# Reordering VectorE's preparing steps, the one-hot and mask step and the sums' transpose in a clustered attention kernel

## The chip, the cores and the metric

The kernel runs on one core of a Trainium2 chip. The metric is the device time of one execution in microseconds. Three runs of the kernel before took 787.32, 787.58 and 790.29 us, so the median is 787.58 us. All times below are microseconds unless ns stands beside them.

## The reference

Attention in which a query sees only the keys of its own cluster, and two dense layers behind it. The core of it:

```python
q_assign = np.argmax(np.einsum('bhsd,hcd->bhsc', q_n, c_n), axis=-1)
k_assign = np.argmax(np.einsum('bhsd,hcd->bhsc', k_n, c_n), axis=-1)
mask = q_assign[:, :, :, None] == k_assign[:, :, None, :]
scores = scale * np.matmul(q, k.transpose(0, 1, 3, 2))
scores = np.where(mask, scores, -1000000000.0)
attn = np.exp(scores - np.max(scores, axis=-1, keepdims=True))
attn = attn / (np.sum(attn, axis=-1, keepdims=True) + 1e-09)
out = np.matmul(attn, v)              # (2, 8, 768, 64)
x = out.transpose(0, 2, 1, 3).reshape(1536, 512)
h = x @ w_in                          # 512 -> 2048
x = softplus(h) @ w_out
h = x @ w_in2
out = (h * clip(h + 3, 0, 6) / 6) @ w_out2
```

There are 2 batches, 8 heads, 768 positions, head size 64 and 16 clusters; `argmax` takes the first of equal values. All of it is float32, and the kernel splits operands into a high and a low part and multiplies the parts.

## The kernel before

The attention works on eight pairs of heads, numbered 0 to 7. A pair takes twelve slots: two heads with six tiles of 128 queries each. In slot s the program issues, in this order: the exp of tile s+1 on ScalarE (line 424), the row maximum of tile s+2 on VectorE (`nm`, 416), the flips of tile s, the scores of tile s+3 on TensorE (408) and a piece of the product with the values (453). A flip is made of transposes of the exponentials on TensorE (`t`, 438) in two halves of three, and behind each half a high part on ScalarE (`pth`, 442) and a low part on VectorE (`ptl`, 443). The halves of `t` lie in two PSUM buffers, so each half waits for the low part of the same half one slot before. The scores have two PSUM buffers, so those of tile s+3 wait for the exp of tile s+1. Behind every third slot ScalarE copies a finished product (`xs`, 466 and 468).

Between these stand the steps that prepare a later pair. Each slot has seven positions, 0 to 6: position 1 lies behind the exp, 2 behind the row maximum, 3 between the two halves of the flip, 4 behind the flips, 5 behind the scores, 6 at the slot's end. A table written by hand, `at(slot, position, step, ...)`, says where each step is issued, and every engine runs its own instructions in that order. For pair n (2 to 7), o is the slot 12n - 12, and the twelve slots around o to o+11 are called the round of pair n here. Pair 1 has lines of its own in the table.

The steps that find a position's cluster: similarities (`psm`, 308), transposed back (`pbk`, 321), the maximum per group (`mx`, 330), equality with it (`eq`, 336), a rank multiplied on by GpSimd (343), the maximum of the ranks (`mx`, 348), the first of them as a one-hot row (`oh`, 353), its transposes on TensorE (`po`, 361), and from them the mask rows on ScalarE (`mk`, 367). `assemble` and `assemble_mask` copy the prepared query and key rows and the mask rows into `Q` and `K` by transfers issued on SP, whose queue also holds the pieces of the dense layers' weights (`fetch_part`). `psm`, `pbk`, `po` and the transposed sums share one PSUM buffer.

The sums of the exponentials of a finished pair are transposed on TensorE (`tot_flip`, `pb`, 483), copied by ScalarE (`tot_out`, `rT`, 488) and sent by SP; GpSimd scales the products by them and splits them into parts (`fin_hi` 511, `fin_lo` 517). GpSimd also splits the values (`p_values`, 377 and 378) and the centroids (290, 291) of the coming pair.

Pair 1's lines put the one-hot step and mask so:

```python
                    at(4, 4, p_first, n)
                    at(5, 3, p_onehot, n)
                    at(5, 6, p_mask, n)
```

Of the kernel before, what the change touches and what calls it, by code (L numbers as in the profile page):

```python
# [22 lines left out]
def cluster_attention_then_two_mlps(  # L23
# [149 lines left out]
    def attention():  # L173
        with ExitStack() as st, ExitStack() as st_ld, ExitStack() as st_ps:
# [347 lines left out]
            def at(s, where, fn, *a):  # L522
                extra.setdefault((s, where), []).append((fn, a))
# [5 lines left out]
            for n in range(NP):  # L529
                o = SL * n - SL  # L530
                if n > 1:
                    at(max(o + -15, 3), 6, load_qk, n, "q")
                    at(max(o + -13, 4), 6, load_qk, n, "k")
                    at(max(o + -9, 4), 5, p_centroids, n)
                    q0 = max(o + -11, 6)
                    at(q0, 1, p_split_hi, n, "q", 0)
                    at(q0, 2, p_split_lo, n, "q", 0)
                    at(o + -5, 1, p_split_hi, n, "q", 1)
                    at(o + -5, 2, p_split_lo, n, "q", 1)
                    at(o + -4, 1, p_split_hi, n, "k", 0)  # L540
                    at(o + -4, 2, p_split_lo, n, "k", 0)
                    at(o + -3, 5, p_split_hi, n, "k", 1)
                    at(o + -2, 1, p_split_lo, n, "k", 1)
                    at(o + -1, 4, p_sims, n, 0)
                    at(o + -1, 4, p_sims, n, 1)
                    at(o + 0, 1, p_sims, n, 2)
                    at(o + 0, 4, p_sims, n, 3)
                    at(o + 0, 4, p_sims_out, n)
                    at(o + 1, 1, p_back, n)
                    at(o + 1, 4, p_max, n)  # L550
                    at(o + 2, 2, p_equal, n)
                    at(o + 2, 4, p_rank, n)
                    at(o + 4, 2, p_best, n)
                    at(o + 5, 2, p_first, n)
                    at(o + 6, 3, p_onehot, n)
                    at(o + 6, 6, p_mask, n)
                    at(o + 4, 1, assemble, n, 0)
                    at(o + 7, 1, assemble_mask, n, 0)
                    at(o + 10, 5, assemble, n, 1)
                    at(o + 11, 4, assemble_mask, n, 1)  # L560
                    at(o + -3, 6, load_v, n)
                    at(o + 5, 5, p_values, n, 0)
                    at(o + 6, 4, p_values, n, 1)
                elif n:
                    at(0, 3, p_sims, n, 2)
                    at(0, 6, p_sims, n, 1)
                    at(1, 3, p_sims, n, 3)
                    at(1, 4, p_sims_out, n)
                    at(2, 3, p_back, n)
                    at(2, 6, p_max, n)  # L570
                    at(3, 2, p_equal, n)
                    at(3, 4, p_rank, n)
                    at(4, 2, p_best, n)
# [3 lines that stand above are left out]
                    at(4, 3, assemble, n, 0)  # L577
                    at(6, 3, assemble_mask, n, 0)
                    at(10, 5, assemble, n, 1)
                    at(11, 4, assemble_mask, n, 1)  # L580
                    at(1, 1, load_v, n)
                    at(7, 0, p_values, n, 0)
                    at(10, 3, p_values, n, 1)
                o += 2 * SL
                if n < NP - 1:
                    at(o + -2, 4, total, n)
                    at(o + 3, 0, tot_flip, n)
                    at(o + 3, 4, tot_out, n)
                    at(o + 4, 4, tot_spread, n)
                    at(o + 9, 4, fin_scale, n, 0)  # L590
                    at(o + 10, 4, fin_scale, n, 1)
                    at(o + 12, 5, fin_hi, n, 0)
                    at(o + 14, 5, fin_hi, n, 1)
                    at(o + 16, 2, fin_lo, n, 0)
                    at(o + 17, 3, fin_lo, n, 1)
                else:
                    at(o + -1, 1, total, n)
                    at(o + 1, 1, tot_flip, n)
                    at(o + 1, 1, tot_out, n)
                    at(o + 1, 5, tot_spread, n)  # L600
                    at(o + 4, 2, fin_scale, n, 0)
                    at(o + 4, 4, fin_hi, n, 0)
                    at(o + 4, 6, fin_lo, n, 0)
                    at(o + 4, 5, fin_scale, n, 1)
                    at(o + 4, 6, fin_hi, n, 1)
                    at(o + 6, 1, fin_lo, n, 1)
# [233 lines left out]
    with tc.manual_schedule():  # L840
        attention()
# [174 lines left out]
```

## Time and profile before

| | |
|---|---|
| time, median of 3 runs | 787.58 |
| time of the profiled execution | 787.78 |
| its span | 786.0 |
| TensorE busy, share of the span | 769.7, 98% |
| VectorE | 459.2, 58% |
| ScalarE | 416.1, 53% |
| GpSimd | 153.4, 20% |
| TensorE waiting for `K<-mk` transfers | 3.3 in 3 waits |

The attention stage takes about the first 260 us; the dense layers follow, and there TensorE runs without a gap that matters. The shares are means over both stages, so what a change in the attention stage does is read from windows and timelines of that stage. A row of a timeline gives start, duration, engine, line, operation, tiles and shapes, and in brackets how long its engine sat idle before it and for what; several alike are merged (x6), and then the duration is that of all of them. Durations of neighbours on one engine overlap a little.

### The profile page before, as it was taken

What the parts mean: (1) busy time and instruction counts of PE and PEld (TensorE: products, weight loads), DVE (VectorE), ACT (ScalarE), POOL (GpSimd) and SP (SyncE); (2) the same over time, 40 slices, a digit from 0 to 9 for tenths busy, and PEclk for the clock granted to TensorE, in tenths of its full rate; (3) what the DMA queues carried; (4) which work ended last, traced back from release to release, by engine and by line L of the source; (5) the groups of instructions that cost most, each with busy time, mean ns of one, the idle gap of its engine ahead of it and who ended that gap; (6) DMA issues with size and microseconds to landing.
All of it is one profiled execution on the core that took longest, in us unless ns stands there. A gap on an engine that the chain in (4) does not pass through costs nothing.

```text
span 786.0 us, 10568 instructions
## 1 busy us (share of the span) xinstructions
PE 769.7 (98%) x3841; PEld 642.6 (82%) x3841; DVE 459.2 (58%) x787; ACT 416.1 (53%) x830; POOL 153.4 (20%) x223
## 2 busy tenths in 40 slices
PE   7899999999999899999999999999999999999998
PEld 6688888898888688888888888888888888888886
DVE  6888878888888999821111267779842322232222
ACT  6898889889899666531212344455532322222221
POOL 4666757757433200000000000000000000000000
PEclk9999999999999999999999999999999999999999
DMA  6658667457372670000000356640000100010001
GB/s 188 168 144 220 148 163 182 106 136 167 86 213 93 218 285 0 1 1 0 1 1 27 106 169 208 189 159 0 1 1 0 54 1 0 1 54 0 1 1 54
DMA packets 39124, 69.75 MB, mean 89 GB/s; under 512 B 4480, under 2 KB 24096, under 8 KB 39072
## 3 DMA queue, kind: packets, MB, share of 16 engines
q1 hardware_dynamic: 39072, 69.08, 30.5%
q8 instruction: 30, 0.49, 0.3%
q14 instruction: 22, 0.18, 0.1%
HBM read 46.30 MB, written 3.19 MB: 63 GB/s over the span
## 4 chain that ended last, share of the span: by engine, by line
PE 84%; ACT 6%; DMA 4%; DVE 3%; issue 1%; SPq 1%; POOL 1%; ACTq 0%; DVEq 0%; POOLq 0%
PE h L169 32%; PE y L892 17%; PE y L890 16%; PE s L408 6%; PE t L438 5%; PE pv L453 5%; ACT pr L424 2%; ACT pth L442 2%; PE psm L308 2%; DMA K<-hik 2%; DMA q<-in_q 1%; DMA K<-mk 1%; SPq L397 1%; DMA Q<-loq 1%; DVE nm L416 0%
## 5 line engine op out<-in xcount | busy, mean ns | idle before, releaser
L169 PE MATMUL h<-xhi,pi 128*128 128x512 f32 x768 | 238.8, 392 | 2.2 <-DVE pi L144 2.2
L169 PEld LDWEIGHTS h<-xhi,pi 128*128 128x128 f32 x768 | 143.7, 188 | 34.3 <-DVE pi L144 3.0
L871 DVE TENSOR_TENSOR glo<-g,ghi 128x512 fp32r<-128x512 f32 x96 | 66.4, 692 | 146.2 <-ACT ghi L858 117.4
L169 PE MATMUL h<-xlo,pi 128*128 128x512 f32 x384 | 150.0, 391 | 0.0
L892 PE MATMUL y<-po,ghi 128*128 128x512 f32 x384 | 118.9, 391 | 0.0
L890 PE MATMUL y<-ghi,po 128*128 128x512 f32 x384 | 118.8, 391 | 0.0
L443 DVE TENSOR_TENSOR ptl<-t,pth 128x384 fp32r<-128x384 f32 x192 | 97.8, 550 | 31.0 <-ACT pth L442 30.6
L864 DVE SCALAR_TENSOR_TENSOR g<-u,h 128x512 f32<-128x512 f32 x48 | 33.0, 688 | 127.1 <-ACT u L860 127.1
L860 ACT ACTIVATE u<-h,half 128x512 f32<-128x512 f32 x48 | 32.9, 686 | 128.3 <-PE h L169 128.0
L408 PE MATMUL s<-K,Q 128*128 128x256 f32 (+1 forms) x384 | 90.8, 357 | 6.0 <-DMA K<-mk 3.3
L442 ACT ACTIVATE pth<-t 128x384 fp32r<-128x384 f32 x192 | 85.1, 487 | 16.8 <-PE t L438 16.2
L416 DVE TENSOR_REDUCE nm<-s 128x1 f32<-128x768 f32 x96 | 90.7, 945 | 4.5 <-PE s L408 4.5
L424 ACT ACTIVATE pr<-s,nm 128x768 f32<-128x768 f32 x96 | 86.5, 902 | 3.4 <-DVE nm L416 3.0
L438 PE MATMUL t<-ident,pr 128*128 128x128 f32 x576 | 87.0, 279 | 0.6 <-DVE ptl L443 0.2
L857 ACT ACTIVATE g<-h 128x512 f32<-128x512 f32 x48 | 28.5, 594 | 110.8 <-PE h L169 110.8
L169 PEld LDWEIGHTS h<-xlo,pi 128*128 128x128 f32 x384 | 72.1, 188 | 15.6
L892 PEld LDWEIGHTS y<-po,ghi 128*128 128x128 f32 x384 | 72.1, 188 | 15.6
L890 PEld LDWEIGHTS y<-ghi,po 128*128 128x128 f32 x384 | 72.0, 188 | 15.6
L408 PEld LDWEIGHTS s<-K,Q 128*128 128x128 f32 x384 | 65.8, 189 | 18.1 <-ACT pr L424 4.9
L438 PEld LDWEIGHTS t<-ident,pr 128*128 128x128 f32 x576 | 64.8, 140 | 17.4 <-DVE ptl L443 13.3
L892 PE MATMUL y<-po,glo 128*128 128x512 f32 x192 | 75.1, 391 | 0.0
L890 PE MATMUL y<-glo,po 128*128 128x512 f32 x192 | 75.0, 391 | 0.0
(123 smaller groups left out, 941.5 us busy)
## 6 DMA issues: line engine op xcount, KB each, us to landing
ri<-in_moe_w_in SPq DMA_DIRECT2D x29, 512.0 KB, 4.7
ro<-in_moe_w_out SPq DMA_DIRECT2D x29, 512.0 KB, 4.5
K<-hik SPq DMA_DIRECT2D x31, 192.0 KB, 4.8
Q<-hiq SPq DMA_DIRECT2D x15, 384.0 KB, 5.0
Q<-loq SPq DMA_DIRECT2D x16, 192.0 KB, 4.3
v<-in_v SPq DMA_DIRECT2D x8, 384.0 KB
rsb<-row SPq DMA_DIRECT2D x16, 192.0 KB, 3.9
out<-o SPq DMA_DIRECT2D x12, 256.0 KB, 2.0
```

The costliest lines, as they stand in the source:

```text
L169: nc.tensor.matmul(hs[n][:, :TB], w[:, c, :], x[c][:, cols], start=(c == 0 and i == 0), stop=(c == NC - 1 and i == 2))
L408: nc.tensor.matmul(ps[:, n0:n1], Q[i][:, u, j * P:(j + 1) * P], K[i][:, u, n0:n1], start=(u == 0), stop=(u == 1),)
L416: nc.vector.tensor_reduce(nm, st_s[t][:, :S], AX.X, ALU.max, negate=True)
L424: nc.scalar.activation(pr, st_s.pop(t)[:, :S], AF.Exp, bias=st_p[t], accum_out=sums_of[n][:, i, j:j + 1])
L438: nc.tensor.transpose(pt[:, c * P:(c + 1) * P], pr[:, kt * P:(kt + 1) * P], ident)
L442: last_flip[:] = [nc.scalar.activation(dh, src, AF.Copy)]
L443: nc.vector.tensor_tensor(dl, src, f32(dh), ALU.subtract)
L453: nc.tensor.matmul(st_v[h][:, :HALF], vs[:, kt, i, :], st_t[h][u][:, kt, :], start=(kt == 0 and u == 0), stop=(kt == NJ - 1 and u == 1),)
L864: nc.vector.scalar_tensor_tensor(t["g"], t["u"], 1.0, t["h"], ALU.min, ALU.mult)
L871: nc.vector.tensor_tensor(t["glo"], t["g"], f32(t["ghi"]), ALU.subtract)
L890: nc.tensor.matmul(y[:, :TB], w[:, e, :], x, **fl)
L892: nc.tensor.matmul(y, x[:, e * P:(e + 1) * P], w.rearrange("p c e -> p (c e)"), **fl)
```

## The change

Nothing is added or taken away; entries of the table move. For pairs 2 to 7 the equality, the maximum of ranks and the first-index step go from position 2, in front of a slot's low parts, to position 4, behind them (the latter two one slot earlier); the rank moves one position on; the one-hot transposes and the mask copy move from slot o+6 to slot o+5, the mask's transfers from (o+7, 1) to (o+6, 3); and the transpose of the sums goes from the head of slot o+3 to behind its scores.

```diff
-                    at(o + 2, 2, p_equal, n)
-                    at(o + 2, 4, p_rank, n)
-                    at(o + 4, 2, p_best, n)
-                    at(o + 5, 2, p_first, n)
-                    at(o + 6, 3, p_onehot, n)
-                    at(o + 6, 6, p_mask, n)
+                    at(o + 2, 4, p_equal, n)
+                    at(o + 2, 5, p_rank, n)
+                    at(o + 3, 4, p_best, n)
+                    at(o + 4, 4, p_first, n)
+                    at(o + 5, 3, p_onehot, n)
+                    at(o + 5, 6, p_mask, n)
...
-                    at(o + 7, 1, assemble_mask, n, 0)
+                    at(o + 6, 3, assemble_mask, n, 0)
...
-                    at(o + 3, 0, tot_flip, n)
-                    at(o + 3, 4, tot_out, n)
+                    at(o + 3, 5, tot_flip, n)
+                    at(o + 3, 6, tot_out, n)
```

On VectorE, this is what stands from slot o+1 (`mx` from `pbk`) to slot o+6 in the round of pair 2 before, with a slot's two low parts in one row:

```order
 L330 TENSOR_REDUCE mx<-pbk 128x24
 L416 TENSOR_REDUCE nm<-s 128x1
+L443 TENSOR_TENSOR ptl<-t,pth 128x3x128 x2
 L336 TENSOR_TENSOR eq<-pbk,mx 128x384
-L443 TENSOR_TENSOR ptl<-t,pth 128x3x128 x2
-L416 TENSOR_REDUCE nm<-s 128x1
-L443 TENSOR_TENSOR ptl<-t,pth 128x3x128 x2
-L416 TENSOR_REDUCE nm<-s 128x1
-L348 TENSOR_REDUCE mx_950<-eq 128x24
-L443 TENSOR_TENSOR ptl<-t,pth 128x3x128 x2
-L416 TENSOR_REDUCE nm<-s 128x1
-L353 TENSOR_TENSOR oh<-eq,mx_950 128x384
```

Rows with a minus are where they stood before: each preparing step lies between a row maximum and the low parts. The rows that follow now:

```order
+L416 TENSOR_REDUCE nm<-s 128x1
+L443 TENSOR_TENSOR ptl<-t,pth 128x3x128 x2
+L348 TENSOR_REDUCE mx_918<-eq 128x24
+L416 TENSOR_REDUCE nm<-s 128x1
+L443 TENSOR_TENSOR ptl<-t,pth 128x3x128 x2
+L353 TENSOR_TENSOR oh<-eq,mx_918 128x384
+L416 TENSOR_REDUCE nm<-s 128x1
```

Each step has changed places with the low parts and the row maximum: it lies behind the low parts and in front of the next row maximum, and `oh` stands one pair of low parts nearer to the start of the round.

On TensorE, slot o+5 of the same round now, from its flips to the values' product (before, its six transposes stood in one row without the `po` rows between them, which came one slot later):

```order
 L438 MATMUL t<-ident,pr 128x128 x3
 L361 LDWEIGHTS oh
 L361 MATMUL po<-identb,oh 128x128
 L361 LDWEIGHTS oh
 L361 MATMUL po<-identb,oh 128x128
 L361 LDWEIGHTS oh
 L361 MATMUL po<-identb,oh 128x128
 L438 MATMUL t<-ident,pr 128x128 x3
 L408 MATMUL s<-K_156,Q_154 128x512 x2
 L408 MATMUL s<-K_156,Q_154 128x256 x2
```

The one-hot transposes of the round stand between the two halves of the flip of slot o+5, one slot earlier than before and one VectorE row behind the step that makes `oh`.

## Rows read from the trace of the kernel before

**Rows 1.** Windows, one round each (engine busy, count; clock, DMA).

```profile
46.74:76.61 29.87, 28.93 (x188) 25.55 (x188) 25.87 (x46) 26.67 (x61) 18.45 (x24) 1.00 0.80 213
76.61:106.21 29.60, 28.90 (x189) 25.57 (x187) 24.46 (x44) 25.84 (x60) 20.21 (x27) 1.00 0.68 172
106.21:135.48 29.27, 29.05 (x188) 25.53 (x187) 24.44 (x44) 25.95 (x61) 20.19 (x27) 1.00 0.64 157
```

**Rows 2.** Timeline, TensorE, round of pair 4 (start, duration).

```profile
117.10 1.01 PE L438 MATMUL t<-ident,pr 128*128 128x128 f32 x6
...
119.38 1.01 PE L438 MATMUL t<-ident,pr 128*128 128x128 f32 x6
...
121.67 0.96 PE L438 MATMUL t<-ident,pr 128*128 128x128 f32 x6
122.09 0.31 PEld L438 LDWEIGHTS t<-ident,pr 128*128 128x128 f32 x3 [0.15 <-DVE ptl L443]
...
127.38 0.97 PE L408 MATMUL s<-K,Q 128*128 128x512 f32 x4 [0.21 <-ACT pr L424]
```

**Rows 3.** Timeline, VectorE, same round.

```profile
116.04 0.55 DVE L336 TENSOR_TENSOR eq<-pbk,mx 128x384 f32<-128x384 f32 x1
116.50 1.01 DVE L443 TENSOR_TENSOR ptl<-t,pth 128x384 fp32r<-128x384 f32 x2
...
119.70 0.95 DVE L416 TENSOR_REDUCE nm<-s 128x1 f32<-128x768 f32 x1
120.57 0.54 DVE L348 TENSOR_REDUCE mx<-eq 128x24 f32<-128x384 f32 x1
121.03 1.01 DVE L443 TENSOR_TENSOR ptl<-t,pth 128x384 fp32r<-128x384 f32 x2
...
122.82 0.55 DVE L353 TENSOR_TENSOR oh<-eq,mx 128x384 bf16<-128x384 f32 x1
```

**Rows 4.** Timeline, ScalarE, same round.

```profile
117.23 0.48 ACT L466 ACTIVATE xs<-pv 64x384 f32<-64x384 f32 x1
...
118.24 0.88 ACT L442 ACTIVATE pth<-t 128x384 fp32r<-128x384 f32 x2
...
122.21 0.96 ACT L442 ACTIVATE pth<-t 128x384 fp32r<-128x384 f32 x2 [0.41 <-PE t L438]
```

**Rows 5.** Timeline, VectorE and TensorE, slots 5 to 7 of round 1.

```profile
31.57 0.55 DVE L353 TENSOR_TENSOR oh<-eq,mx 128x384 bf16<-128x384 f32 x1
...
32.17 0.17 PEld L361 LDWEIGHTS <-oh 128*128 128x128 bf16 x3 [0.29 <-DVE oh L353]
...
32.35 0.50 PE L438 MATMUL t<-ident,pr 128*128 128x128 f32 x3
...
37.62 0.95 PE L408 MATMUL s<-K,Q 128*128 128x512 f32 x4
```

**Rows 6.** Timeline, GpSimd, round of pair 4.

```profile
116.67 1.00 POOL L343 TENSOR_TENSOR eq<-eq,tiew 128x384 f32<-128x384 f32 x1 [1.81 <-DVE eq L336]
117.61 0.50 POOL L511 CAST xhi<-xs 128x384 fp32r<-128x384 f32 x1
118.29 1.01 POOL L471 TENSOR_TENSOR xs<-xs,xs 128x384 f32<-128x384 f32 x1 [0.18 <-ACT xs L468]
...
120.36 1.99 POOL L517 TENSOR_TENSOR xlo<-xs,xhi 128x384 fp32r<-128x384 f32 x2
...
122.88 1.37 POOL L378 TENSOR_TENSOR vs<-v,vs 128x384 fp32r<-128x384 f32 x1
```

**Rows 7.** Timeline, GpSimd and VectorE, round of pair 7.

```profile
210.52 0.51 POOL L377 CAST vs<-v 128x384 fp32r<-128x384 f32 x1
210.63 0.81 DVE L353 TENSOR_TENSOR oh<-eq,mx 128x384 bf16<-128x384 f32 x1
```

**Rows 8.** TensorE's waits over the span (total, times, longest).

```profile
PE s L408 <- DMA K<-mk: 3.3, 3, 2.1
```

**Rows 9.** Timeline, SP's queue in round 3.

```profile
97.34 1.55 SPq L102 DMA_DIRECT2D ro<-in_moe_w_out  x3
```

## The prediction

> **What bounds the kernel now.** I read the page first: TensorE is nearly never idle, and after about 260 us its order is untouched by the change, so only the attention stage can move. Then I cut that stage at the same instruction of successive rounds with the windows view. A round (twelve slots, one head pair) takes 29.87, 29.60 and 29.27 us [rows 1]; ScalarE is busy for 25.95 of the last and VectorE for 24.44, so neither is full, and the granted clock is 1.00 throughout. The reader should see that the first two rounds are longer by 0.60 and 0.33 though their work is the same: these are the rounds in which scores wait for a mask transfer [rows 8]. Third, the timeline of one round, engine by engine. Below I use the round of pair 4: the flips of its slots o+3, o+4 and o+5 start at 117.10, 119.38 and 121.67, the scores of slot o+7 at 127.38 [rows 2]. A flip (the transposes of line 438) needs the PSUM half that VectorE's low part of the slot before has read, and low parts need ScalarE's high parts. The loop TensorE, ScalarE, VectorE, TensorE is what ends each slot, and the wait that ends last changes from slot to slot.
>
> **The change part by part.** It adds and removes no instruction. Six rounds change, those of pairs 2 to 7; pair 1 has lines of its own.
>
> *Equality, rank and second maximum behind the low parts.* Before, `eq` at 116.04 held up the low parts at 116.50 [rows 3], and the flips of slot o+3 were stretched to 1.01, waiting 0.36 for them [rows 2]. Now the low parts start 0.46 earlier and that stretch should go. It is worth nothing, because what is late next is in the same slot: ScalarE's two `xs` copies from 117.23 hold the high parts until 118.24 [rows 4], whatever VectorE does, and the low parts behind them release the flips at 119.38 [rows 2] as before. I take 0 per round; if that cover were absent it would be 0.36. One slot on, `mx` moves ahead of the row maximum, and the order becomes 0.46 of `mx`, 0.87 of `nm`, low parts, the same sum between two low parts: they stay at 121.03 [rows 3]. The row maximum ends 0.46 later, and the exp that reads it can be late by that at most; ScalarE idled 0.41 right behind that exp [rows 4], so this is hidden but for 0.05. `eq` starts 0.93 later, behind the low parts, and so does the rank on GpSimd: it ends at 116.67 + 0.93 + 1.00 = 118.60 [rows 6], over 1 us before `mx` asks for it at 119.70.
>
> *The sums' transpose behind the scores.* It costs TensorE the same, one place later. ScalarE's copy `rT` stands behind high parts that start at 118.24 and take 0.88 [rows 4]; by their end the flips and scores of the slot are long through, and the transpose with them. 0; SP's row transfer and the queue behind it start as before. Had ScalarE to wait, exp and the flips behind it would be late by what is missing of one transpose, a few tenths.
>
> *First-index and one-hot one slot earlier.* This is where I find the cost. Each VectorE row starts some 0.08 before the one ahead of it ends. `oh` now stands directly behind the low parts of slot o+4, so it starts at 121.03 + 1.01 - 0.08 = 121.96 instead of 122.82 and ends 0.55 later, at 122.51 [rows 3]. But its transposes moved by a whole slot, between the two flips of slot o+5. The second flip was free to go at 122.09 [rows 2]; now it stands behind transposes that wait for `oh`. Round 1 already has this arrangement and shows its price: `oh` from 31.57 ends at 32.12, TensorE waits 0.29 for it, and the second flip goes at 32.35, 0.23 behind the end of `oh` [rows 5]. So here: 122.51 + 0.23 = 122.74, against 122.09, 0.65 late. Does it come back? ScalarE has no slack from there on: `xs` and mask copy fall between this flip and the scores of slot o+7, in either order. Before, the way from the second flip to those scores took 127.38 - 122.09 = 5.29; in round 1, with the mask copy where the change puts it, 37.62 - 32.35 = 5.27 [rows 2, 5]. Equal, so the flip's lateness arrives whole. Six rounds: 6 x 0.65 = 3.9. Bounds: 0 if `oh` is there in time, 0.65 plus what follows if not.
>
> *What `oh` meets there.* `oh` reads two SBUF tensors. In round 7 it took 0.81 instead of 0.55: a cast on GpSimd had begun 0.11 earlier, and `oh` ended 0.41 behind the cast's end, as if it had stood still until then [rows 7]. In the other order, `oh` at 122.82 and GpSimd's L378 at 122.88, it was L378 that took 1.37, where the rank took 1.00 for the same size [rows 6]. So whichever starts second waits. At its new place `oh` meets the pair of L517 instructions: 120.36 to 122.35 before [rows 6]. The rank's delay moves them: rank to 118.60, then the addition (which waited for ScalarE until 118.29), then the pair, about 0.3 later, 120.6 to 122.6. `oh` at 121.96 falls inside the second one and waits until 122.6, ends at 123.0 instead of 122.5: 0.5 more for the flip, all of it on the same path. The pair stands there in the rounds of pairs 3 to 6; in that of pair 2 a short cast stands there, and in that of pair 7 the small centroid splits are missing, so the pair is through earlier. Bounds 0 (a gap) and 1.0 (all of one L517) a round; I take 0.5 for four and 0.2 for two, an estimate nearest to the row of round 7: 2.4.
>
> The Trainium skill ("SBUF — State Buffer", section "Who interferes with whom") says that a VectorE instruction with two SBUF inputs contends with a GpSimd instruction that reads SBUF, since its second input comes through a shared read interface, and that who issues first holds it for the whole instruction. By that rule the sum keeps the 2.4, without it it loses them; rows 6 and 7 agree with it in both directions.
>
> *Mask one slot earlier, and its transfers ahead of one weight piece.* In rounds 2 and 3 the mask's transfers stood behind three weight transfers that took SP 1.55 [rows 9], not behind the mask copy; one of the three now goes behind them, so masks land about 0.5 earlier while TensorE comes later by the above. Those waits go, and what shows is the undisturbed round: 0.60 + 0.33 = 0.9 gained [rows 1]. The wait of 2.1 in rows 8 belongs to round 1 and stays. In rounds 4 to 7 nothing waited there: 0.
>
> Sum: +3.9 + 2.4 - 0.9 = +5.4. The profiled execution took 787.78 (span 786.0 and 1.78 around it), 0.2 above the median shown, 787.58. From that median: 793.0.
>
> **The rivals.**
> A. The wait for `oh` comes, the meeting with GpSimd does not (the two slip past each other by a few tenths): +3.9 - 0.9 = +3.0, 790.6. For it: GpSimd's place is worked out over five instructions. Against it: `oh` is 0.4 inside the second L517 and 0.6 ahead of its end.
> B. The other side, not slower: the low parts no longer stand behind the preparing steps, and VectorE gets ahead so far that `oh` ends before the first flip of slot o+5 does, near 122.1. Then the stretch of 0.36 in six rounds and the 0.9 of mask waits are gained: -2.2 - 0.9 = -3.1, 784.5. It decides at `oh` starting 0.4 earlier than I put it. For it: three of the four steps do leave the low parts' way. Against it: `xs` at 117.23 fixes when the low parts of slot o+3 can start, and the chain behind is VectorE without a gap.
> C. The mask copy ahead of exp counts a second time: exp and with it the scores of slot o+6 come 0.56 later, and those of o+7 once more. +0.56 in six rounds on top: 5.4 + 3.4 = +8.8, 796.4. Against it: the equal 5.29 and 5.27.
>
> **How the numbers follow.** My forecast gets 0.50, A 0.32, B 0.10, C 0.08. For A the range must reach down to 789, for half of C and for a full meeting in all rounds (0.5 more in five) up to 795.5; below lies B with a bit of A, above most of C. Half a per cent, 3.9 us, is about what a measurement of this kernel can tell from no change; the bounds are 783.6 and 791.5. Slower: nine tenths of my forecast, a fifth of A, all of C, 0.59. Faster: a third of B and little else, 0.04. The rest, 0.37, is the same.
>
> **What would show it.** In the changed profile, round 4: flips of slot o+3 no longer stretched, yet those of o+4 where they were; a new TensorE wait for `oh` in rounds 2 to 7, 0.6 to 1.1 each between two flips of slot o+5; `oh` at about 1.0 instead of 0.55 in four rounds and starting during an L517; no wait of scores for `K<-mk` but round 1's; rounds of about 30.4. `oh` at 0.55 means A, no wait for `oh` means B, and then I was wrong; scores of slot o+6 waiting 0.5 for exp mean C.

## The result, and the profile after

The changed kernel took 794.22 us (median of 5 runs, 792.47 to 795.57), the kernel before 787.81 beside it (5 runs, 787.32 to 790.29). The ratio is 1.0068 with a 95% interval of 1.0052 to 1.0083, so the change costs 5.4 us (4.1 to 6.5); the two medians lie 6.4 apart, at the upper end of that. The prediction was 793.0 in a range of 789.0 to 795.5, slower the likeliest. The profiled execution took 792.47 with a span of 790.7, 4.7 more than the one of before.

The windows of rounds 2, 3, 4 and 7, cut at the same instruction as [rows 1]:

```profile
46.50:76.61 30.11, 29.38 (x188) 25.59 (x187) 26.00 (x46) 27.04 (x62) 18.37 (x24) 1.00 0.78 207
76.61:107.01 30.40, 29.32 (x188) 25.71 (x187) 24.90 (x43) 26.20 (x61) 20.02 (x27) 1.00 0.69 177
107.01:137.37 30.36, 29.28 (x188) 25.69 (x187) 24.88 (x43) 26.20 (x61) 20.05 (x27) 1.00 0.61 148
198.10:227.96 29.86, 29.28 (x188) 25.70 (x187) 24.38 (x43) 26.20 (x61) 11.06 (x13) 1.00 0.47 100
```

Against [rows 1] rounds 2, 3 and 4 are 0.24, 0.80 and 1.09 longer. Rounds 5 and 6 cut the same way are 1.10 longer each, round 7 (29.27 before) 0.59. Together 4.92. The stretch ahead of them is 0.24 shorter, which leaves 4.7: the whole difference of the two spans.

TensorE's waits over the span (total, times, longest):

```profile
PE po L361 <- DVE oh L353: 4.6, 6, 0.9
...
PE s L408 <- DMA K<-mk: 1.9, 1, 1.9
```

The wait for `oh` is new, one in each of six rounds: 0.64 in round 2, 0.89 or 0.90 in rounds 3 to 6, and 0.38 in round 7, where the prediction said 0.6 at least. Of the three waits of [rows 8] only round 1's is left. TensorE in the round of pair 4, against [rows 2]:

```profile
117.63 0.82 PE L438 MATMUL t<-ident,pr 128*128 128x128 f32 x6
...
120.18 1.01 PE L438 MATMUL t<-ident,pr 128*128 128x128 f32 x6
...
122.47 0.51 PE L438 MATMUL t<-ident,pr 128*128 128x128 f32 x3
123.86 0.34 PE L361 MATMUL po<-identb,oh 128*128 128x128 bf16 x3 [0.89 <-DVE oh L353]
...
123.99 0.31 PEld L438 LDWEIGHTS t<-ident,pr 128*128 128x128 f32 x3
...
129.31 0.94 PE L408 MATMUL s<-K,Q 128*128 128x512 f32 x4
```

The flips of slot o+3 are no longer stretched (0.82 for 1.01). Those of o+4 still are, and stand where they stood: 120.18 is 119.38 plus the 0.80 by which the round starts later. In slot o+5 the one-hot transposes stand between the halves and wait 0.89, and the second half goes at 123.99. That is 1.10 behind its place before (122.09 + 0.80). From there to the scores of slot o+7 it takes 5.32, 5.29 before: the lateness arrives whole, within 0.03. VectorE, same round, against [rows 3], with the one-hot of rounds 2 and 7 around it:

```profile
62.26 0.80 DVE L353 TENSOR_TENSOR oh<-eq,mx 128x384 bf16<-128x384 f32 x1
...
117.77 0.54 DVE L336 TENSOR_TENSOR eq<-pbk,mx 128x384 f32<-128x384 f32 x1
...
120.50 0.54 DVE L348 TENSOR_REDUCE mx<-eq 128x24 f32<-128x384 f32 x1
120.96 0.95 DVE L416 TENSOR_REDUCE nm<-s 128x1 f32<-128x768 f32 x1
121.83 1.01 DVE L443 TENSOR_TENSOR ptl<-t,pth 128x384 fp32r<-128x384 f32 x2
122.75 1.05 DVE L353 TENSOR_TENSOR oh<-eq,mx 128x384 bf16<-128x384 f32 x1
123.73 0.94 DVE L416 TENSOR_REDUCE nm<-s 128x1 f32<-128x768 f32 x1
...
213.85 0.55 DVE L353 TENSOR_TENSOR oh<-eq,mx 128x384 bf16<-128x384 f32 x1
```

The one-hot takes 1.05 in round 4 (1.06 in rounds 3, 5 and 6), 0.80 in round 2 and 0.55 in round 7. GpSimd, rounds 4 and 7, against [rows 6]:

```profile
118.39 1.01 POOL L343 TENSOR_TENSOR eq<-eq,tiew 128x384 f32<-128x384 f32 x1 [2.30 <-DVE eq L336]
119.36 1.01 POOL L471 TENSOR_TENSOR xs<-xs,xs 128x384 f32<-128x384 f32 x1
...
121.41 1.98 POOL L517 TENSOR_TENSOR xlo<-xs,xhi 128x384 fp32r<-128x384 f32 x2
123.33 0.83 POOL L377 CAST vs<-v 128x384 fp32r<-128x384 f32 x1
...
211.43 1.98 POOL L517 TENSOR_TENSOR xlo<-xs,xhi 128x384 fp32r<-128x384 f32 x2
213.35 0.51 POOL L377 CAST vs<-v 128x384 fp32r<-128x384 f32 x1
213.93 1.33 POOL L378 TENSOR_TENSOR vs<-v,vs 128x384 fp32r<-128x384 f32 x1
```

The pair of L517 ends at 121.41 + 1.98 = 123.39. The one-hot, begun at 122.75, ends at 123.80, 0.41 behind that, the distance of [rows 7]. The cast behind the pair, 0.51 otherwise, takes 0.83: it waits for the one-hot in its turn. In round 7 the pair is through at 213.41, before the one-hot begins at 213.85; there the one-hot is first, and it is L378, begun at 213.93, that takes 1.33, where the rank took 1.01. ScalarE, round 4, against [rows 4]:

```profile
118.03 0.48 ACT L466 ACTIVATE xs<-pv 64x384 f32<-64x384 f32 x1
...
119.04 0.87 ACT L442 ACTIVATE pth<-t 128x384 fp32r<-128x384 f32 x2
...
122.00 0.90 ACT L424 ACTIVATE pr<-s,nm 128x768 f32<-128x768 f32 x1 [0.28 <-DVE nm L416]
...
124.58 0.49 ACT L442 ACTIVATE pth<-t 128x384 fp32r<-128x384 f32 x1 [1.07 <-PE t L438]
...
125.52 0.90 ACT L424 ACTIVATE pr<-s,nm 128x768 f32<-128x768 f32 x1
```

`xs` and the high parts behind it stand 0.80 later than before, so the cover named for slot o+3 was there. The exp now waits 0.28 for the row maximum behind `mx`, and the idle 0.41 that followed it is gone. What is new is 1.07 for the second half of the flip. SP in round 3, against [rows 9]:

```profile
97.29 1.06 SPq L102 DMA_DIRECT2D ro<-in_moe_w_out  x2
98.44 1.20 SPq L397 DMA_DIRECT2D Q<-mk  x2
99.69 1.22 SPq L397 DMA_DIRECT2D K<-mk  x2
100.95 0.58 SPq L102 DMA_DIRECT2D ro<-in_moe_w_out  x1
```

One of the three weight pieces has gone behind the mask's transfers, as worked out.

### The profile page after: what moved, and what is told of

It reads as the page before. It is cut to its first block, busy times and chain, and to the rows that moved or that the text cites. A ratio compares the mean times of both kernels' runs of the same rounds, so it can differ in the third digit from the quotient of the medians.

```text
span 790.7 us, 10574 instructions
## 1 busy us (share of the span) xinstructions
PE 771.3 (98%) x3841; PEld 643.7 (81%) x3841; DVE 460.6 (58%) x787; ACT 418.0 (53%) x830; POOL 153.2 (19%) x223
## 4 chain that ended last, share of the span: by engine, by line
PE 85%; ACT 7%; DVE 6%; issue 1%; POOL 0%; DMA 0%; SPq 0%; ACTq 0%; DVEq 0%; POOLq 0%
PE h L169 32%; PE y L892 17%; PE y L890 16%; PE pv L453 6%; PE t L438 6%; PE s L408 5%; ACT pth L442 2%; PE psm L308 2%; ACT pr L424 2%; DVE ptl L443 2%; ACT xs L468 1%; DVE nm L416 1%; DVE oh L353 1%; ACT xs L466 1%; PE warm L245 0%
## 5 line engine op out<-in xcount | busy, mean ns | idle before, releaser
L438 PE MATMUL t<-ident,pr 128*128 128x128 f32 x576 | 85.4, 277 | 1.2 <-DVE ptl L443 0.2
```

The source lines that it names most:

```text
L438: nc.tensor.transpose(pt[:, c * P:(c + 1) * P], pr[:, kt * P:(kt + 1) * P], ident)
```

## The experiments

Each was timed in turn with the kernel before on the same chip, and its ratio is to that. Rounds are cut here from the first similarities (`psm`) of one to the next, from each kernel's profiled execution; rounds 5 to 7 are not in the table. The ratios also hold the clock dip told of at the end, which falls in round 1 of some executions; the rounds of the table lie behind it.

| kernel | rounds 2, 3, 4 | ratio | 95% interval |
|---|---|---|---|
| before | 29.82, 29.59, 29.27 | | |
| changed | 30.11, 30.39, 30.36 | 1.0068 | 1.0052 to 1.0083 |
| one-hot back | 29.85, 30.13, 30.10 | 1.0038 | 1.0026 to 1.0051 |
| one-hot alone | 30.75, 30.76, 30.73 | 1.0095 | 1.0081 to 1.0109 |
| sums alone | 29.84, 29.49, 29.27 | 0.9997 | 0.9986 to 1.0009 |
| centroids behind | 30.13, 29.89, 29.87 | 1.0037 | 1.0022 to 1.0051 |
| one-hot behind scores | 29.75, 29.78, 29.77 | 1.0044 | 1.0031 to 1.0056 |
| back, centroids behind | 29.92, 29.61, 29.60 | 1.0023 | 1.0010 to 1.0035 |
| mask on VectorE | 29.95, 29.73, 28.88 | 0.9994 | 0.9985 to 1.0004 |
| combined | 28.90, 28.89, 28.92 | 0.9973 | 0.9963 to 0.9984 |
| combined, values later | 28.91, 28.89, 28.89 | 0.9959 | 0.9945 to 0.9972 |
| values later alone | 29.81, 29.52, 29.27 | 0.9981 | 0.9972 to 0.9989 |

**One-hot back.** The changed kernel, with the one-hot's transposes, the mask and its transfers where they were.

```diff
-                    at(o + 5, 3, p_onehot, n)
-                    at(o + 5, 6, p_mask, n)
+                    at(o + 6, 3, p_onehot, n)
+                    at(o + 6, 6, p_mask, n)
...
-                    at(o + 6, 3, assemble_mask, n, 0)
+                    at(o + 7, 1, assemble_mask, n, 0)
```

> The changed kernel with the one-hot transposes, the mask copy and the mask's transfers back in slots o+6 and o+7; VectorE's preparing steps stay behind the low parts, the sums' transpose behind the scores. Theory 1 (the cost is TensorE's wait for the first-index step between two flips, and only that): no wait of po for oh in rounds 2 to 7, mask waits of rounds 2 and 3 as before, the time of the kernel before, 787.8, ratio 1.000. Theory 2 (oh in front of the row maximum, and held up by GpSimd, is a second path of nearly the same length: the row maximum of slot o+5 ends 0.8 later, the exp that reads it starts at about the row maximum's end + 0.1 instead of 123.06, and ScalarE has no slack behind it): rounds 4 to 6 longer than 29.27 by 0.7 to 0.9, round 7 by 0.4, in round 2 the lateness hides in the mask wait; together +3 to +4, 791, ratio 1.004. Oh still takes 1.05 in rounds 3 to 6 in both.

The ratio is 1.0038: no wait for `oh` is left, and yet rounds 4 to 6 are 0.83 to 0.86 longer than before. Its timelines, VectorE and then ScalarE, round 4:

```profile
122.58 1.06 DVE L353 TENSOR_TENSOR oh<-eq,mx 128x384 bf16<-128x384 f32 x1
123.57 0.94 DVE L416 TENSOR_REDUCE nm<-s 128x1 f32<-128x768 f32 x1
```

```profile
121.83 0.90 ACT L424 ACTIVATE pr<-s,nm 128x768 f32<-128x768 f32 x1 [0.29 <-DVE nm L416]
...
124.61 0.90 ACT L424 ACTIVATE pr<-s,nm 128x768 f32<-128x768 f32 x1 [0.81 <-DVE nm L416]
```

This is a second path, which the prediction does not have (the expectation names it). The one-hot now stands ahead of a row maximum, that maximum ends late, and the next exp waits 0.81 for it. ScalarE idles 0.29 + 0.81 = 1.10 in this stretch, 0.41 before [rows 4], so 0.69 of the 0.83 is there.

**One-hot alone.** The kernel before with only the three lines of that diff, in the other direction: one-hot, mask and transfers one slot earlier.

> The kernel before with only the one-hot transposes, the mask copy and the mask's transfers one slot earlier. Theory 1 (the second flip of slot o+5 starts 0.23 behind the end of oh, and its lateness arrives whole): oh stays at 122.82 to 123.37 of round 4, the flip goes at 123.6 instead of 122.09, each of six rounds 1.5 longer, less 0.9 for the mask waits of rounds 2 and 3: +8, 796, ratio 1.010; po waits for oh about 1.2 six times. Rival (what costs is VectorE's steps behind the low parts and the meeting with GpSimd; the one-hot transposes alone are short and TensorE catches up): within 1 us of the kernel before, 787 to 789, and oh at 0.55 as before in both.

1.0095, as expected. Without the earlier `mx` and first-index step the one-hot comes later, and TensorE, round 4 of this kernel, waits longer for it:

```profile
125.69 0.34 PE L361 MATMUL po<-identb,oh 128*128 128x128 bf16 x3 [1.25 <-DVE oh L353]
```

Rounds 4 to 6 are 1.46 longer than before, 1.10 in the changed kernel. So the moved VectorE steps soften what the one-hot's move costs, by 0.36 a round; moved without it they cost 0.83, as one-hot back shows. The two costs do not add.

**Sums alone.** The kernel before with only the last two lines of the change.

> The kernel before with only the sums' transpose and its copy behind the scores of slot o+3. My working: 0; ScalarE never waits for the transpose, rounds of 29.27 stay, 787.8, ratio 1.000 within 0.001. Rival (the copy rT now waits for TensorE and everything on ScalarE behind it, and SP's row transfer and mask transfers behind that, come later): a ScalarE wait of rT on pb of some tenths in each round, +1 to +2 in all.

0.9997: nothing that the interval can tell, as expected.

**Centroids behind.** The changed kernel with GpSimd's four short centroid splits two slots later, so that the pair L517 is through before the one-hot begins.

```diff
-                    at(max(o + -9, 4), 5, p_centroids, n)
+                    at(max(o + -7, 4), 4, p_centroids, n)
```

> The changed kernel with the centroid splits of the next pair moved behind the two low parts of the outputs on GpSimd, so that these end about 1.1 earlier and short operations of about 0.2 stand where oh comes; the other engines keep their order. Theory of the shared path (oh waits while a GpSimd instruction that began first runs): oh falls from 1.05 to 0.55 to 0.75 in rounds 3 to 6, po waits 0.4 to 0.6 there instead of 0.9, each of the four rounds 0.35 to 0.5 shorter: 1.4 to 2.0 less than the changed kernel, rounds 4 to 6 at 29.9 to 30.0 instead of 30.37, ratio to before about 1.0045. Rival (oh is long because of what it reads or because of its place behind the low parts): oh stays at 1.05 and rounds at 30.37, ratio 1.0068.

1.0037, a little less than expected. GpSimd, VectorE and TensorE in its round 4:

```profile
120.69 1.99 POOL L517 TENSOR_TENSOR xlo<-xs,xhi 128x384 fp32r<-128x384 f32 x2
```

```profile
123.12 0.55 DVE L353 TENSOR_TENSOR oh<-eq,mx 128x384 bf16<-128x384 f32 x1
```

```profile
123.73 0.34 PE L361 MATMUL po<-identb,oh 128*128 128x128 bf16 x3 [0.39 <-DVE oh L353]
```

The one-hot takes 0.55 again, TensorE's wait falls from 0.89 to 0.39, and rounds 4 to 6 are 0.48 or 0.49 shorter than in the changed kernel. That is the meeting, by itself. What is left over the kernel before, 0.60 to 0.62 in each of these rounds, goes with the place of the one-hot and its transposes.

**One-hot behind the scores.** The changed kernel with the transposes two positions later.

```diff
-                    at(o + 5, 3, p_onehot, n)
+                    at(o + 5, 5, p_onehot, n)
```

> The changed kernel with the one-hot one step later only, behind the scores of its slot, so that the transposed one-hot is copied by ScalarE where it is copied in the changed kernel. Theory (two paths: TensorE's wait for the one-hot, and the exp of slot o+6 that comes behind the late row maximum): no wait of po for oh is left, but the maximum still comes behind the one-hot, at about 124.0 against 123.1 before, so that rounds 4 to 7 take about 29.6 us (before 29.27): some 1.2 to 1.4 us over the kernel before, ratio 1.0015. Rival (the earlier place of the mask's copy on ScalarE is the cost): rounds stay near 30.4, ratio 1.007. Rival (only the wait of po costs anything): ratio 1.000.

1.0044: missed, it should have been 1.0015. Rounds 4 to 6 are 0.50 longer than before where 0.35 was expected, and ScalarE in round 5 shows a wait that the expectation does not have:

```profile
156.25 0.67 ACT L367 ACTIVATE mk<-po,mbi,msc 128x384 fp32r<-128x384 bf16 x1 [0.40 <-PE po L361]
```

Behind the scores the transposes are late for the mask's copy, and ScalarE waits for them instead. Round 7, cut at its flips, is 0.52 longer, so the rounds account for about 2.1 us of the 3.5. The rest goes with the clock dip told of below: 5 of the 6 runs have a mean clock of 0.998 or less, and the sixth took 789.86, 2.0 over the runs of the kernel before that have more (median 787.88). The rival that the earlier mask copy is the cost falls: it is as early here as in the changed kernel, and the rounds are 0.6 shorter.

**Back, centroids behind.** Both edits at once: one-hot back, centroids two slots later.

> The changed kernel with the one-hot's transposes, the mask and its transfers put back where the kernel before has them (as in e1_onehot_back), and besides GpSimd's work on the centroids moved two slots later (as in e4_centroids_behind), so that the one-hot no longer begins during a GpSimd instruction. Theory: the one-hot takes 0.55 us instead of 1.06, so that the row maximum behind it is 0.5 less late: rounds 4 to 7 of about 29.65 us, ratio 1.002, against 1.0038 without the second move. Rival (the maximum's lateness is not what costs e1 its 3 us): ratio 1.0038 again.

1.0023, as expected: rounds 4 to 6 are 0.30 to 0.33 longer than before, 0.5 less than without the centroids' move. The late row maximum is shown as the second path: shorten the one-hot ahead of it, and the round gets that much shorter. Against centroids behind (0.60 to 0.62) it also shows what the earlier place of transposes and mask adds to that path: 0.3 a round (0.26, changed kernel against one-hot back, where the one-hot takes 1.06).

**Mask on VectorE.** The kernel before with the mask made by VectorE from round 2 on, and the two steps at earlier positions of the same slot (the expectation says that nothing else moves; these positions do).

```diff
-                nc.scalar.activation(mk, d["po"][:, :HALF], AF.Identity, bias=mbi, scale=msc)
+                if n < 2:
+                    nc.scalar.activation(mk, d["po"][:, :HALF], AF.Identity, bias=mbi, scale=msc)
+                else:
+                    nc.vector.tensor_scalar(mk, d["po"][:, :HALF], msc, mbi, ALU.mult, ALU.add)
...
-                    at(o + 6, 3, p_onehot, n)
-                    at(o + 6, 6, p_mask, n)
+                    at(o + 6, 1, p_onehot, n)
+                    at(o + 6, 2, p_mask, n)
```

> The kernel before with the transposed one-hot copied (and made into the mask) by VectorE instead of ScalarE from round 2 on, nothing else moved. It asks whether ScalarE has slack in a round. Theory (it has none, its 29.27 us are the round): rounds 4 to 7 become shorter by part of that copy's 0.67, to about 28.8; rounds 2 and 3 stay as they are, bound by the mask's transfers; about 1.7 us less than the kernel before, ratio 0.998. Rival (TensorE or VectorE sets the round): rounds of 29.3 or more, ratio 1.000 or above.

0.9994, and the interval holds 1: the total decides nothing. The rounds do: 4 to 6 are 0.36 to 0.39 shorter, near the expected 28.8, and 2 and 3 are 0.13 and 0.14 longer. The windows of rounds 3 and 5 of this kernel:

```profile
79.50:109.20 29.70, 28.66 (x189) 25.46 (x188) 24.93 (x44) 25.41 (x59) 20.18 (x27) 1.00 0.70 176
138.10:167.00 28.90, 28.89 (x189) 25.44 (x188) 24.84 (x45) 25.54 (x60) 20.15 (x27) 1.00 0.61 146
```

With that copy gone from ScalarE, TensorE is busy for 28.89 of 28.90. So ScalarE had no slack for that copy where it stood; the copy's engine and its place changed together, and no run parts them. That TensorE now sets the round is read from its busy time alone, which was already 29.05 of 29.27 [rows 1].

**Combined.** The last kernel, with the mask's transfers right behind the mask and three weight pieces behind them.

```diff
-                    at(o + 7, 1, assemble_mask, n, 0)
+                    at(o + 6, 3, assemble_mask, n, 0)
...
-                        at(12 * f + 6 * e + c - 2, 0, fetch_part, 0, f, nm, c)
+                        at(12 * f + 9 * e + c - 2, 0, fetch_part, 0, f, nm, c)
```

> A version that may beat both: the kernel before with the mask's copy on VectorE (as in e6_mask_on_vector), the mask's transfers issued right behind it, and the fetches of three weight pieces of each round put behind those transfers. Theory (ScalarE sets rounds 4 to 7, the mask's transfers rounds 2 and 3): all of rounds 2 to 7 near 28.9 us, some 3.4 us less than the kernel before, ratio 0.9957. Rival: ratio 1.000 or above.

0.9973: faster than both kernels, less so than expected, though rounds 2 to 6 are at 28.9 as expected. Here too the clock dip has a part: 8 of the 11 runs have a mean clock of 0.998 or less, and the other three have a median of 784.86, 3.0 under the runs of the kernel before that have more. Round 4 of it:

```profile
103.40:132.30 28.90, 28.89 (x188) 25.43 (x188) 24.82 (x45) 25.54 (x59) 20.19 (x27) 1.00 0.65 165
```

**Values later, combined and alone.** The load of pair 1's values stands ahead of round 1's first mask transfers on SP's queue. It moves behind them, once in the combined kernel and once in the kernel before.

```diff
-                    at(1, 1, load_v, n)
+                    at(1, 3, load_v, n)
```

> e10_combined with one more transfer moved: the load of pair 1's values, which stands on SP's queue ahead of the first mask transfers of round 1, now behind them. In e10_combined those scores wait 1.85 us for K<-mk. Theory: the load waits for its buffer and holds the mask's transfers up, so the wait goes: some 1.9 us less than e10_combined in every run, and besides no dip of TensorE's granted clock after that wait, so that all runs have a mean clock of 0.999 or more and lie within 2 us of each other: ratio to the kernel before 0.9945. Rival: the wait moves to the next transfer in the queue, ratio 0.997 as e10_combined.

> The kernel before with only that load moved behind the first mask transfers of round 1. Runs of the kernel before spread over 787.3 to 792.0 us, with mean granted clocks of 1.000 to 0.995; in executions with the lower mean the clock dips to about 0.8 right behind TensorE's wait of 2.1 us for K<-mk in round 1. Theory (the idle wait brings the dip): without the wait no run dips, median some 2.5 to 3 us lower, ratio 0.9965, and a spread under 2 us. Rival (the dip has another cause): about 2 us less, but spread and mean clocks as before, ratio 0.9975.

0.9959 and 0.9981. SP's queue, in the kernel before and then with the load moved:

```profile
23.21 0.34 SPq L212 DMA_DIRECT2D v<-in_v  x1
23.66 1.19 SPq L397 DMA_DIRECT2D Q<-mk  x2
```

```profile
21.39 1.19 SPq L397 DMA_DIRECT2D Q<-mk  x2
...
24.56 0.38 SPq L212 DMA_DIRECT2D v<-in_v  x1
```

The mask's transfers go 2.27 earlier and round 1's wait of 2.1 is gone. The gain of the median is less than expected in both (1.5 instead of 2.5 to 3 in the kernel before), since round 2 then starts only 1.28 earlier in the profile. In the combined kernel the wait itself gave less still: without it the profiled execution's span is 782.7, with it 783.0. The clocks came out as the theory had them (below). The combined kernel with it is the best here: 785.01 against 788.57 of the kernel before in the same job.

## Why the prediction was right, and where it was not

- *Equality and rank behind the low parts: 0.* The rows stand as it says, though no run moves these steps alone: the stretch of slot o+3 goes, `xs` covers it, and the flips of slot o+4 stand where they stood. The rank ends at 119.40, 1.1 before `mx`.
- *Row maximum behind `mx`: hidden.* Right: 0.28 of waiting took the place of 0.41 idle behind that exp.
- *Sums' transpose: 0.* Shown by the run of it alone (0.9997).
- *Waiting for the one-hot: +0.65 a round, not given back.* Near: 0.60 to 0.62 without the meeting, and 5.32 behind 5.29 from the late flip to the scores of slot o+7. That same number is against rival C. The 0.05 too much is a reading, told below the list.
- *The meeting with GpSimd: +0.5 in four rounds, +0.2 in two.* Shown for the four: moving the centroid splits takes 0.48 or 0.49 a round away. In round 2 the one-hot took 0.25 longer. In round 7 nothing held it up: there the term was 0 instead of 0.2, though the text itself says that the pair is through earlier in that round. The Trainium skill ("SBUF — State Buffer", section "Who interferes with whom") has it that a VectorE instruction with two SBUF inputs contends with a GpSimd instruction that reads SBUF, and that issue order decides who blocks. The rows agree: 1.05 where L517 was first, 0.83 for the cast behind it where the one-hot was first, 0.55 where they do not meet.
- *Mask transfers: -0.9.* Two waits gone, as said. Round 2 came out at +0.24 (0.65 + 0.2 - 0.60 = 0.25) and round 3 at +0.80 (0.65 + 0.5 - 0.33 = 0.82).

The reading: 122.09 of [rows 2] starts a weight load of the flip, but 32.35 of [rows 5] starts its matmuls. Round 1's weight load starts 0.05 earlier:

```profile
32.30 0.31 PEld L438 LDWEIGHTS t<-ident,pr 128*128 128x128 f32 x3
```

Like for like, the flip goes 0.18 behind the one-hot's end. That gives 0.60 a round, and 5.32 for the way to the scores, just what the changed kernel shows.

The sum was +5.4. The profiled rounds give 4.9 (the difference is nearly all round 7 and 0.05 in each of three rounds). That the ratio gives 5.4 to the tenth is chance, with an interval of 4.1 to 6.5.

**What it had wrong** is the bound below: "0 if `oh` is there in time". The one-hot stands ahead of a row maximum now, and the prediction followed that delay for `mx` only. One-hot back shows what this costs: 0.83 a round though nothing waits for `oh`, and 0.3 even where the one-hot takes 0.55. In the changed kernel that lateness lies beside TensorE's wait: the row maximum ends at 123.73 + 0.94 = 124.67, but the exp comes at 125.52, behind the late flip's high part and the mask's copy. So the two are not added, and the sum came out because the path that it follows is the longer one. The prediction did not weigh the two: in that it was lucky. Putting the transposes back gives only 0.26 of the 1.10 a round, since the second path is left. Rival B (a one-hot that ends by 122.1) did not come about, and no run makes it; its gain of 3.1 stays untested.

What stays open: of the 0.83, 0.69 is seen as ScalarE's idle time; the last 0.14 is not laid to a row.

## What to carry to other kernels

Behind a step that moves, look at everything that now stands behind it on its engine: here the one-hot held up both the transposes that read it and the row maximum that does not. Several waits into one loop overlap, so take one away and the next shows; a part's cost is known only when it is run alone, and when it is taken out. When an engine is busy for 26 of 29 us and yet sets the loop, look for work on it that another engine can do: giving one copy of 0.67 to VectorE shortened the rounds by 0.4, while every reordering of the preparing steps alone left rounds 4 to 6 as they were or lengthened them. (The copy's place in the slot changed too.)

## What the runs showed of the hardware

TensorE's granted clock can dip after a short wait, in some executions and not in others. In round 1 TensorE waits about 2 us for mask transfers (2.05 in the mask-on-VectorE kernel). Windows of that kernel at that place, and then of the values-later kernel:

```profile
26.00:30.00 4.00, 1.95 (x8) 1.57 (x9) 2.60 (x6) 1.95 (x5) 1.76 (x5) 0.82 0.63 172
30.00:34.00 4.00, 4.00 (x22) 3.63 (x22) 2.97 (x6) 2.13 (x4) 1.86 (x2) 0.76 0.92 247
```

```profile
26.00:30.00 4.00, 3.70 (x23) 2.93 (x21) 4.00 (x8) 2.84 (x7) 1.77 (x5) 1.00 0.89 289
30.00:34.00 4.00, 3.62 (x27) 3.00 (x26) 4.00 (x8) 3.95 (x9) 2.93 (x3) 1.00 1.06 255
```

In the first, TensorE was busy for 1.95 of the 4 us that hold the wait, and the clock was at its lower level (1.2 GHz) for part of these 8 us: 0.82 and 0.76 on average. A matmul of the values took 0.52 there, 0.34 at the same place in the kernel before (L456 is that kernel's 453):

```profile
29.71 0.52 PE L456 MATMUL pv<-pth,vs 128*128 128x384 f32 x1
```

The profiled execution of the kernel before has the same wait without a dip, so the wait alone does not decide it:

```profile
26.00:30.00 4.00, 1.93 (x13) 1.62 (x12) 3.07 (x6) 1.55 (x4) 1.76 (x5) 1.00 0.65 165
```

Of 26 runs of the kernel before in one job, 11 had a mean clock of 0.998 or less over the span and a median of 789.35; the other 15 had 787.88. With the wait gone (load moved), all 11 runs of the one kernel and all 5 of the other had 0.999 or more, while 5 of the 15 runs of the kernel before beside them had 0.998 or less. In the job of the first four experiments it was 10 of 15. So by the profiled executions this wait costs 1.28 us in the kernel before and 0.3 in the combined one, and the runs with the lower mean clock are about 1.5 longer still; this is a large part of what spreads the runs of the kernel before. What else decides whether an execution dips is not shown.
